# The second transform stage taken four chunks at a time, with its row swaps replaced by other matmuls, and one output tile required between wide groups

## The chip, the cores and the metric

The kernel runs on one core of a Trainium2 chip. The metric is the device time of one execution in microseconds, as a median of several runs. One execution was also recorded by the hardware profiler; its own time stands beside the others in the table below.

## What is computed

Two branches read the same normalized input and are added to it:

```python
xn = _layernorm(x, axis=-1)                      # x: 1 x 2048 x 576
return x + _A_ref(xn, k, v, shift_k, ssm_k, ssm_D) + _B_ref(xn, w1, w2)

# _A_ref: a short causal convolution of k, times v, then a causal convolution
# over all 2048 positions for each of 576 channels, then times xn
kv = k_shift * v
y_f = rfft(pad(kv)) * rfft(pad(ssm_k))
y = irfft(y_f)[:S] + kv * ssm_D
return q * y

# _B_ref
h = jnp.maximum(jnp.einsum("bsd,df->bsf", x, w1), 0)   # 576 -> 4608
return jnp.einsum("bsf,fd->bsd", h, w2)                # 4608 -> 576
```

## The kernel before

**The dense branch is the frame.** It runs in 36 steps called quads (18 blocks of 256 hidden columns, for each of two halves of the tokens). A quad consists of products into two PSUM banks (`psh`, 128 x 512, line 569 for every matmul of this branch) and of eight *units* (`mm2`): twelve matmuls of 288 columns into one of two double banks (`pso`), which VectorE then adds to the accumulator of a token tile (line 749). The values are split into a high and a low part, so each product takes three matmuls of the type fp32r. ScalarE makes the high part of activations (`hh`, line 591) and weights (line 512), VectorE the low part of the activations (`ll`, line 593), GpSimd that of the weights (line 513).

**The convolution branch is a stream beside it.** `conv()` is a generator. After every product and unit, `tick` adds to a clock of the dense branch and, at a rate set by `SHARE` and by the planned costs `W_...` and counts `N_...`, lets the generator run on to its next `yield`. So the place of each convolution step among the dense matmuls is fixed by these numbers when the program is built. A step whose matmuls need four PSUM banks yields "wide" first and then may start only at a tick with `place`, which is one behind a product and not one behind a unit. Two of its banks are `psf` (a pool of two), the other two are lent by `borrowed()`: the double bank of the unit that was closed last (`psg`). VectorE must have added that unit to its accumulator before a matmul may write there.

The long convolution is a transform in two stages of sizes 64 and 32, the product with the transformed filter, and the way back. First the filter (`zk`) and then the input (`zx`) go through the first stage into DRAM; then comes the **second stage**, which the change rewrites; last the output stage reads `zy`.

**The second stage before.** Its data are 36 chunks of 128 rows (2 groups of 32 real and 32 imaginary rows) by 512 columns. It takes them in 18 pairs. The constant `m_sb` is a 64 x 64 matrix, one for the way ahead and one for the way back; `turn` multiplies a pair by it with four matmuls of 64 x 64 x 512, each in its own quarter of TensorE's array. For each pair there are three turns: of the filter (`spectrum`, into `psg`), of the input (into `psf`), and the way back (into `psf`). A product of complex numbers needs each real row beside its imaginary row: ScalarE copies the filter twice (line 1020), four DMAs swap half the rows (line 1025), VectorE multiplies in four operations (line 1047), four DMAs swap half the rows of one product (line 1052), and VectorE joins the two with a sign per row in one operation of 1024 columns (line 1059, `join`). The way back follows one pair later, with two copies by ScalarE (line 1067) and two stores (line 1068). Loads of the next chunks (line 1000) and all the swaps go through the queue of SyncE.

Here a *visit* is a stretch of convolution matmuls (line 762) between dense ones. The first and the second turn of the same pair step stand in one visit, the way back in a visit of its own. All order on TensorE is fixed by `in_turn` and `matmuls`; `here()` places operations of ScalarE and VectorE behind the last ones of the dense branch.

The convolution's matmuls are plain fp32, and each shows in the trace as two MATMUL records.

Of the kernel before, what the change touches and what calls it, by code (L numbers as in the profile page):

```python
# [17 lines left out]
P = 128  # L18
S = 2048
D = 576  # L20
# [28 lines left out]
PAUSE = 16000  # L49
PLAIN = 3  # L50
PAUSES = 7.5
SHARE = 0.935


CW = 512
# [5 lines left out]
W_FB, W_FS, W_FK, W_FX, W_FMK, W_FMX, W_FMB, W_FO = 2.8, 4.1, 2.5, 1.75, 4.0, 3.6, 2.9, 3.9  # L61
CONV_TOTAL = (N_FB * W_FB + N_FS * W_FS + N_FK * W_FK + N_FX * W_FX + N_FM * (W_FMK + W_FMX + W_FMB)
              + N_FO * W_FO)


# [1 line left out]
ROWS = 2 * KS + 8  # L67
REST = ROWS * D
Z, KSO, WT = REST, REST + 4 * CW, REST + 4 * CW + 4 * NH
AREA = WT + 4 * U * P  # L70
# [5 lines left out]
def transform_constants():  # L76
# [16 lines left out]
    back = ahead.T  # L93
    mid = np.tile(np.stack([ahead, back], axis=1), (GR, 1, 1)).astype(np.float32)
    return (fwd.reshape(T, P, U, P), inv.reshape(T, P, U, A1),
            np.ascontiguousarray(mid))

# [2 lines left out]
def h3_ffn_kernel(ctx: ExitStack, tc, x, k, v, shift_k, ssm_k, ssm_D, w1, w2, fwd, inv, mid, out):  # L100
# [39 lines left out]
    def fft_psum():  # L140
        return ps_f.tile([P, 512], F32, tag="f", name="psf")

    slot = {"open": 0, "closed": 0}
# [580 lines left out]
    def mm2(g, b, i):  # L724
# [5 lines left out]
        cols = slice(i * P, (i + 1) * P)  # L730
        ps, slot["closed"] = open_ps.pop((g, t))
        unwritten.discard(slot["closed"])
        for h in range(2):
# [26 lines left out]
    def in_turn(ps, a, m, start, stop):  # L760
        with tc.issue_after(done["pe"].ins):
            done["pe"] = nc.tensor.matmul(ps, a, m, start=start, stop=stop, skip_group_check=True)  # L762

    sides = (slice(0, 64), slice(64, P))

    class Ring:

# [30 lines left out]
    def stages(view, views):  # L798
# [164 lines left out]
        for t in range(T):  # L963
            for n in range(KS + 1):
# [8 lines left out]
                if n == 1 or t == T - 1 and n == KS:  # L973
# [6 lines left out]
                    if n == 1 and 2 <= t + 1 < T:  # L980
# [1 line left out]


        stage["seeded"] = ()
        pairs_n = range(NCH // 2)
        raw = {"k": Ring(*views(0, 2, 2, CW)), "x": Ring(*views(ROWS // 2 * D, 2, 2, CW))}
        m_sb = view(8 * CW, 2, 2 * A2)
        filters = Ring(view(4 * CW, 2, 2, CW), view(ROWS // 2 * D + 4 * CW, 2, 2, CW),
                       view(REST + CW, 2, 2, CW))
        other = view(REST - CW, 2, CW)  # L990
        backs = Ring(*views(REST + 5 * CW, 3, CW))
        nc.gpsimd.dma_start(m_sb, mid)

        def both(z, n):
            return z.rearrange("q t g d -> (q t) (g d)")[
                :, 2 * n * CW:2 * (n + 1) * CW].rearrange("p (k n) -> p k n", k=2)

        def load(z, n, name):
            if n in pairs_n:
                nc.sync.dma_start(raw[name].put(n), both(z, n))  # L1000

        def turn(banks, terms):


            for i, (d, src) in enumerate(terms):
                for k in range(2):
                    for r in range(2):
                        in_turn(banks[k][sides[r ^ k]], m_sb[sides[r], d, :],
                                src[sides[r], k, :], i == 0, i == len(terms) - 1)

        def spectrum(n, banks, copied):

            turn(banks, [(0, raw["k"][n])])
            filt = filters.put(n)

            def leave():
                for c in range(2):
                    for dst, src in copied(filt[:, c]):
                        with here():
                            nc.scalar.activation(dst, src, AF.Copy)  # L1020
                for c in range(2):
                    for r in range(2):
                        a = 64 * r + A2 * c
                        b = 64 * r + A2 * (1 - c)
                        nc.sync.dma_start(filt[b:b + A2, c], filt[a:a + A2, c])
                load(zk, n + 2, "k")

            return leave

        def first_spectrum():  # L1030
            banks = [fft_psum() for _ in range(2)]
            spectrum(0, banks, lambda to: [(to[:, k, :], banks[k]) for k in range(2)])()

        def second_spectrum(n):
            wide = borrowed()
            return spectrum(n, [wide[:, k, :] for k in range(2)], lambda to: [(to, wide)])

        def product_of(n):

            banks = [fft_psum() for _ in range(2)]  # L1040
            turn(banks, [(0, raw["x"][n])])
            filt = filters[n]
            leave = second_spectrum(n + 1) if n + 1 in pairs_n else lambda: None
            for c in (1, 0):
                for k in range(2):
                    with here():
                        nc.vector.tensor_tensor(filt[:, c, k, :], banks[k], filt[:, c, k, :],  # L1047
                                                OP.mult)
                if c:
                    for a in range(0, P, A2):  # L1050
                        b = a ^ A2
                        nc.sync.dma_start(other[b:b + A2], filt[a:a + A2, c])
            leave()
            load(zx, n + 2, "x")

        def join(n):
            filt = filters[n][:, 0]
            with here():
                nc.vector.scalar_tensor_tensor(filt, other, sign, filt, op0=OP.mult, op1=OP.add)

        def way_back(n):
            banks = [fft_psum() for _ in range(2)]
            turn(banks, [(1, filters[n][:, 0])])
            for k in range(2):
                vo = backs.put((n, k))
                with here():
                    nc.scalar.activation(vo, banks[k], AF.Copy)
                nc.sync.dma_start(both(zy, n)[:, k, :], vo)

        for n in range(2):  # L1070
            load(zk, n, "k")
        for n in range(2):
            load(zx, n, "x")
        yield -PAUSE
        first_spectrum()
        yield W_FMK
        for n in range(NCH // 2 + 1):
            if n + 1 in pairs_n:
                yield "wide"
            if n:  # L1080
                join(n - 1)
            if n in pairs_n:
                product_of(n)
            yield W_FMK / 2 + W_FMX
            if n:
                way_back(n - 1)
                yield W_FMK / 2 + W_FMB


        order = [*range(HT, T), *range(HT)]  # L1090
# [78 lines left out]
    def tick(cost, place=True):  # L1169
# [134 lines left out]
```

## Time and profile before

| | |
|---|---|
| median of 3 runs | 1029.08 us (1028.98 to 1030.45) |
| the profiled execution | 1038.15 us, of which 1036.3 us are the span of its instructions |
| mean granted TensorE clock | 0.996 |
| busy: TensorE, VectorE, ScalarE, GpSimd | 1019.9, 702.4, 431.4, 463.6 us |
| second stage: first to last of its matmuls | 672.8 to 920.9 us |
| 690 to 920 us: busy TensorE, VectorE, ScalarE, GpSimd | 228.25, 146.91, 102.18, 83.00 us |
| 690 to 920 us: mean busy share of the DMA engines | 0.81, against 0.56 from 480 to 690 us |
| row swaps by DMA | 144, of 128 KB each |

A row of a timeline gives the start and the length in us, the engine, the line, the operation, its output and input by the program's names, the shape, and how many records were merged; in brackets the idle time before it and what ended that. A row of the groups gives busy time and mean ns of one behind the bar. A row of waits gives the total in us, how often, and the longest. Matmuls overlap, so the distance from one start to the next says what a matmul costs; its length does not.

### The profile page before, as it was taken

Reading aid. Unit: us, or ns where it says so; the run is one execution under the profiler, and the core shown is the slowest. Engines: PE = TensorE matmul, PEld = TensorE weight load, DVE = VectorE, ACT = ScalarE, POOL = GpSimd, SP = SyncE. Lnnn points to the kernel's source line nnn. Section 1 sums busy time; section 2 is a strip of 40 time slices with the busy share of each in tenths; the row PEclk is TensorE's granted clock in tenths of the full one; section 3 lists DMA queues with packets and bytes.
Section 4 is the critical chain, followed back from the end, with each engine's and each line's share of the span. In section 5 each row is a group of like instructions: output and inputs, shape, how many; then the busy total and the mean of one; then the engine's idle time right before and its main releaser. Section 6 shows DMA issues by size and latency. Waiting matters only on the chain.

```text
span 1036.3 us, 17434 instructions
## 1 busy us (share of the span) xinstructions
PE 1019.9 (98%) x6506; PEld 846.6 (82%) x6506; DVE 702.4 (68%) x1075; ACT 431.4 (42%) x770; POOL 463.6 (45%) x502
## 2 busy tenths in 40 slices
PE   8999999999999999989999999999999999999997
PEld 5898999998988888878878888866777777788777
DVE  6787677775565556778787889455666666556764
ACT  7244334443354444434444444544444445332120
POOL 3335444555443555544555455314424245244450
PEclk9999999999999999998999999999999999999999
DMA  7114364479445473379944433677877887757684
GB/s 175 52 49 118 114 162 126 154 216 199 115 127 172 160 245 104 126 216 322 277 139 132 129 103 115 210 221 227 242 212 226 250 256 226 221 177 230 208 259 114
DMA packets 130848, 184.69 MB, mean 178 GB/s; under 512 B 69213, under 2 KB 81631, under 8 KB 129868
## 3 DMA queue, kind: packets, MB, share of 16 engines
q1 hardware_dynamic: 76180, 123.48, 39.9%
q0 software_dynamic: 16048, 52.44, 16.9%
q10 hardware_dynamic: 38536, 7.66, 3.9%
q8 instruction: 51, 0.84, 0.3%
q14 instruction: 33, 0.27, 0.1%
HBM read 119.04 MB, written 45.61 MB: 159 GB/s over the span
## 4 chain that ended last, share of the span: by engine, by line
PE 88%; DMA 4%; DVE 3%; ACT 2%; issue 1%; POOL 1%; ACTq 1%; SPq 0%; DVEq 0%; POOLq 0%
PE pso L569 40%; PE psh L569 34%; PE psf L762 6%; PE psg L762 4%; PE psh_c L569 3%; DMA r<-in_w 2%; DMA zk<-area 1%; DMA acc<-in_x 1%; ACTq L809 0%; DVE area L1047 0%; DVE area L941 0%; DVE area L942 0%; ACT x L291 0%; DMA area<-in_k 0%; DVE sums L525 0%
## 5 line engine op out<-in xcount | busy, mean ns | idle before, releaser
L569 PE MATMUL pso<-w,hh 128*128 128x288 f32 x2304 | 467.9, 296 | 0.0
L569 PEld LDWEIGHTS pso<-w,hh 128*128 128x128 f32 x2304 | 378.1, 188 | 35.9 <-issue 14.8
L569 PE MATMUL pso<-w,ll 128*128 128x288 f32 x1152 | 339.5, 295 | 0.0
L749 DVE TENSOR_TENSOR acc<-pso,acc 128x576 f32<-128x576 f32 x243 | 183.1, 754 | 167.3 <-PE pso L569 166.9
L569 PEld LDWEIGHTS pso<-w,ll 128*128 128x128 f32 x1152 | 216.4, 188 | 0.0
L513 POOL TENSOR_TENSOR wb<-sums,wb 128x512 fp32r<-128x512 f32 x33 | 52.4, 1587 | 251.1 <-ACT wb L512 217.9
L513 POOL TENSOR_TENSOR w<-r,w 128x576 fp32r<-128x576 f32 x72 | 108.2, 1510 | 118.6 <-ACT w L512 118.6
L569 PE MATMUL psh<-xs,wb 128*128 128x512 f32 x396 | 102.7, 394 | 0.0
L569 PE MATMUL psh<-x,wa 128*128 128x512 f32 x396 | 102.5, 394 | 0.1
L569 PE MATMUL psh<-hl,wr 128*128 128x512 f32 x264 | 85.7, 406 | 3.6 <-ACT psh L686 3.1
L569 PEld LDWEIGHTS psh<-x,wa 128*128 128x128 f32 x396 | 72.4, 188 | 15.3 <-ACT psh L648 0.5
L569 PEld LDWEIGHTS psh<-xs,wb 128*128 128x128 f32 x396 | 70.6, 188 | 14.6 <-issue 3.2
L513 POOL TENSOR_TENSOR wa<-r,wa 128x512 fp32r<-128x512 f32 x36 | 56.1, 1558 | 57.2 <-ACT wa L512 57.1
L762 PE MATMUL psf<-area 64*64 64x512 f32 (+10 forms) x664 | 75.2, 489 | 1.6 <-DVE area L1047 1.0
L593 DVE SCALAR_TENSOR_TENSOR ll<-psh,hh 128x512 fp32r<-128x512 f32 x66 | 45.2, 685 | 37.6 <-ACT hh L591 37.2
L686 ACT ACTIVATE psh<-psh 128x512 f32<-128x512 f32 x33 | 19.2, 582 | 116.5 <-DVE u L684 114.6
L569 PEld LDWEIGHTS psh<-hl,wr 128*128 128x128 f32 x264 | 46.3, 189 | 23.0 <-issue 10.5
L591 ACT ACTIVATE hh<-psh 128x512 fp32r<-128x512 f32 x66 | 39.3, 596 | 50.8 <-PE psh L569 50.1
L1020 ACT ACTIVATE area<-psg 128x1024 f32<-128x1024 f32 x34 | 33.0, 1024 | 53.7 <-PE psg L762 53.7
L591 ACT ACTIVATE hh<-p 128x512 fp32r<-128x512 f32 x33 | 20.9, 632 | 81.9 <-PE pso L569 46.9
L569 PE MATMUL psh<-xs,wd 128*128 128x512 f32 x198 | 52.6, 401 | 0.0
L1047 DVE TENSOR_TENSOR area<-psf,area 128x512 f32<-128x512 f32 x72 | 44.7, 682 | 11.6 <-DMA area<-area 8.4
(134 smaller groups left out, 1487.0 us busy)
## 6 DMA issues: line engine op xcount, KB each, us to landing
r<-in_w POOLq DMA_DIRECT2D x70, 288.0 KB, 3.8
area<-area SPq DMA_DIRECT2D x144, 128.0 KB, 4.0
r<-in_w POOLq DMA_DIRECT2D x35, 512.0 KB, 4.8
zk<-area SPq DMA_DIRECT2D x64, 144.0 KB, 2.2
area<-zk SPq DMA_DIRECT2D x18, 512.0 KB, 4.5
area<-zx SPq DMA_DIRECT2D x18, 512.0 KB, 4.1
zy<-area SPq DMA_DIRECT2D x36, 256.0 KB, 4.7
area<-zy SPq DMA_DIRECT2D x32, 288.0 KB, 4.3
```

Source lines behind the costliest of these rows:

```text
L513: nc.gpsimd.tensor_tensor(w[:, 1, :n], src, w[:, 0, :n], OP.subtract)
L569: last = nc.tensor.matmul(ps, a, m, start=start and n == 0, stop=n == len(seq) - 1, skip_group_check=True)
L591: done["act"] = nc.scalar.activation(hh, ps, AF.Relu)
L593: nc.vector.scalar_tensor_tensor(ll, ps, 0.0, hh, op0=OP.max, op1=OP.subtract)
L686: nc.scalar.activation(x, y, AF.Copy, scale=-1.0)
L749: done["acc"] = nc.vector.tensor_tensor(two(acc[t]), ps[:, :, :NH], two(acc[t]), OP.add)
L762: done["pe"] = nc.tensor.matmul(ps, a, m, start=start, stop=stop, skip_group_check=True)
L1020: nc.scalar.activation(dst, src, AF.Copy)
L1047: nc.vector.tensor_tensor(filt[:, c, k, :], banks[k], filt[:, c, k, :], OP.mult)
```

## The change

The second stage takes four chunks at a time, nine times. Real and imaginary rows no longer share a tile: `ahead` makes, for each half of the rows (64 partitions) and each of four chunks, the 32 real results (c = 0) and the 32 imaginary ones (c = 1) with two matmuls of 64 x 32 x 512. The four chunks fill the 128 partitions of a bank, and so the real parts lie in one bank and the imaginary parts in another, for each half. The swaps, the second copy of the filter, `sign` and the DMAs of lines 1025 and 1052 are no longer used. The product is then four multiplications (`times`, for a half) and two additions (`joined`); `way_back` accumulates two matmuls of 32 x 64 x 512 in a bank. The imaginary and real part of the second half of the input are copied to SBUF (`xs`), so that its multiplications read SBUF alone; those of the first half read PSUM. A step of four is spread over eight planned pieces of `W_FM`, and their total, 9 x 8 x 2.625, equals the total before, 18 x (4.0 + 3.6 + 2.9). Loads are twice as large and half as many.

All three kinds of visit (input ahead, filter ahead, way back) now need four banks. `SHARE` goes from 0.935 to 0.942, which moves every step of the stream to slightly later ticks. `tick` lets a wide group start only if a unit has been closed since the last loan.

```diff
-SHARE = 0.935
+SHARE = 0.942
-N_FB, N_FS, N_FK, N_FX, N_FM, N_FO = 23, 14, A2, T * (2 * KS + 1) + 2, NCH // 2, T
+N_FB, N_FS, N_FK, N_FX, N_FM, N_FO = 23, 14, A2, T * (2 * KS + 1) + 2, NCH // 4, T
...
     def borrowed():
+        slot["lent"] = slot["units"]
         return ps_o.tile([P, 2, 512], F32, tag=f"o{slot['closed']}", name="psg")
...
+        def ahead(name):
+            narrow, wide = four_banks()
+            banks = narrow, [wide[:, c, :] for c in range(2)]
+            for c in range(2):
+                for k in range(4):
                     for r in range(2):
+                        in_turn(banks[r][c][quarters[k], :],
+                                m_sb[sides[r], 0, A2 * c:A2 * c + A2],
+                                raw[name][sides[r], k, :], True, True)
+            return narrow, wide
...
+        def times(n, r, x, c):
+            filt = filters[n]
+            to = [spec[:, r, i, :] for i in range(2)] if c == 0 else [filt[:, r, i, :]
+                                                                      for i in range(2)]
+            for i in range(2):
+                with here():
+                    nc.vector.tensor_tensor(to[i], x, filt[:, r, i, :], OP.mult)
+
+        def joined(n, r):
+            filt = filters[n]
+            for i, op in enumerate((OP.subtract, OP.add)):
+                with here():
+                    nc.vector.tensor_tensor(spec[:, r, i, :], spec[:, r, i, :],
+                                            filt[:, r, 1 - i, :], op)
+
+        def way_back(n):
+            narrow, wide = four_banks()
+            banks = [*narrow, wide[:, 0, :], wide[:, 1, :]]
+            for c in range(2):
+                for k in range(4):
                     for r in range(2):
+                        in_turn(banks[k][sides[r], :], m_sb[quarters[k], 1 + c, :],
+                                spec[quarters[k], r, c, :], c == 0, c == 1)
+            leave((back[:, 0:2], back[:, 2:4]), narrow, wide)
...
+        for n in fours:
+            yield "wide"
+            narrow, wide = ahead("x")
             with here():
+                nc.scalar.activation(xs, wide, AF.Copy)
+            load(zx, n + 1, "x")
+            for c in range(2):
+                times(n, 0, narrow[c], c)
+                yield W_FM
+            joined(n, 0)
+            yield W_FM
+            if n + 1 in fours:
                 yield "wide"
+                spectrum(n + 1)
+                yield W_FM
+            for c in range(2):
+                times(n, 1, xs[:, c, :], c)
+                yield W_FM
+            joined(n, 1)
+            yield W_FM * (1 if n + 1 in fours else 2)
+            yield "wide"
+            way_back(n)
+            yield W_FM
...
-        while steps and clock["conv"] >= 0 and (place or not clock["wide"]):
+        while steps and clock["conv"] >= 0 and (
+                not clock["wide"] or place and slot["units"] > slot["lent"]):
```

What this does to TensorE's order is seen in quad 27 of the second stage. These are TensorE's rows before, from a way back (two `psf` banks, four matmuls) to the next input and filter; `psh27_...` are dense products, and the rows of the units `pso26_...` that lie between are marked by dots:

```order
L569 MATMUL psh27_5_7696<-xs1_4842,wc27_7598 128x512 x3
L762 MATMUL psf_7700<-area_1173 64x512 x2
L762 MATMUL psf_7701<-area_1173 64x512 x2
L569 MATMUL psh27_5_7696<-xs1_4842,wc27_7598 128x512 x3
...
L569 MATMUL psh27_5_7696<-hl2_4911,wr27_7532 128x512 x2
L762 MATMUL psf_7751<-area_1173 64x512 x2
L762 MATMUL psf_7752<-area_1173 64x512 x2
L762 MATMUL psg_7757<-area_1173 64x512 x4
L569 MATMUL psh27_5_7696<-xs4_4922,wd27_7529 128x512 x6
```

And TensorE's rows of the changed program in the same quad, from a way back (eight matmuls in two rounds) over one unit to an input ahead, of which the first two rows are shown (lines 571 and 765 are 569 and 762 of before):

```order
L765 MATMUL psf_7584<-area_1173 64x512 x2
L765 MATMUL psf_7585<-area_1173 64x512 x2
L765 MATMUL psg_7583<-area_1173 64x512 x4
L765 MATMUL psf_7584<-area_1173 64x512 x2
L765 MATMUL psf_7585<-area_1173 64x512 x2
L765 MATMUL psg_7583<-area_1173 64x512 x4
L571 MATMUL psh27_1_7536<-hl2_4910,wr27_7500 128x512 x2
L571 MATMUL pso26_10_7563<-w226_7299,hh26_0_0_7281 128x288 x2
...
L571 MATMUL psh27_2_7537<-xs2_4812,wb27_7494 128x512 x6
L765 MATMUL psf_7639<-area_1173 32x512
L765 MATMUL psg_7638<-area_1173 32x512
```

Before, a lent bank (`psg`) was first written in the second turn of a visit, behind the two `psf` banks; in the changed program the second matmul of an input ahead writes it already, and a way back needs it in its first round. In the whole program there were 64 visits, and now there are 55: 27 in place of 36 belong to the second stage.

ScalarE's rows in the changed program behind that way back are these (line 1026 is the copy out of the second stage's banks, 593 makes `hh`, 665 copies a dense bank, 1071 is the copy into `xs`):

```order
L1026 ACTIVATE area_1173<-psf_7584 128x512
L1026 ACTIVATE area_1173<-psf_7585 128x512
L1026 ACTIVATE area_1173<-psg_7583 128x1024
L593 ACTIVATE hh27_0_0_7609<-psh27_1_7536 128x512
...
L1071 ACTIVATE area_1173<-psg_7638 128x1024
```

Before, `hh27_0_0` stood behind two copies of `psf` and two of `psg`, as the following rows of ScalarE before show:

```order
L1067 ACTIVATE area_1173<-psf_7573 128x512
L1067 ACTIVATE area_1173<-psf_7574 128x512
L1020 ACTIVATE area_1173<-psg_7628 128x1024 x2
L591 ACTIVATE hh27_0_0_7651<-psh27_1_7564 128x512
```

VectorE's rows before, at the same place (line 749 adds a unit to its accumulator, 593 makes `ll`):

```order
L1059 SCALAR_TENSOR_TENSOR area_1173<-area_1173,sign_85 128x1024
L1047 TENSOR_TENSOR area_1173<-psf_7622,area_1173 128x512 x2
L1047 TENSOR_TENSOR area_1173<-psf_7623,area_1173 128x512 x2
L749 TENSOR_TENSOR acc10_5124<-pso26_10_7601,acc10_5124 128x576
L593 SCALAR_TENSOR_TENSOR ll27_0_0_7652<-psh27_1_7564,hh27_0_0_7651 128x512
L749 TENSOR_TENSOR acc10_5124<-pso26_11_7655,acc10_5124 128x576
```

And these are VectorE's rows of the changed program there and on to the next way back (line 752 adds a unit to its accumulator, 595 makes `ll`, 1040 is `times`, 1046 `joined`, 693 adds a dense bank):

```order
L595 SCALAR_TENSOR_TENSOR ll27_0_0_7610<-psh27_1_7536,hh27_0_0_7609 128x512
L752 TENSOR_TENSOR acc10_5121<-pso26_10_7563,acc10_5121 128x576
L1040 TENSOR_TENSOR area_1173<-psf_7639,area_1173 128x512 x2
L1040 TENSOR_TENSOR area_1173<-psf_7640,area_1173 128x512 x2
L752 TENSOR_TENSOR acc10_5121<-pso26_11_7613,acc10_5121 128x576
...
L752 TENSOR_TENSOR acc14_5257<-pso26_14_7765,acc14_5257 128x576
L595 SCALAR_TENSOR_TENSOR ll27_0_1_7762<-u2_27_7663,hh27_0_1_7761 128x512
L1046 TENSOR_TENSOR area_1173<-area_1173 128x512 x2
L693 TENSOR_TENSOR p5_27_7711<-psh27_2_7537,p5_27_7711 128x512
L752 TENSOR_TENSOR acc14_5257<-pso26_15_7779,acc14_5257 128x576
```

The accumulation of a unit whose bank is lent next stands here behind `ll`, products and sums of the second stage, in the order of VectorE's queue.

More of the change, by code (lines that the diff above doesn't have):

```diff
@@ L732, in mm2 @@
         unwritten.discard(slot["closed"])
+        slot["units"] += 1
         for h in range(2):
@@ L764, in h3_ffn_kernel @@
     sides = (slice(0, 64), slice(64, P))
+    quarters = [slice(a, a + A2) for a in range(0, P, A2)]
     class Ring:
@@ L984, in stages @@
         stage["seeded"] = ()
[L985 to L991, printed above, removed]
+        fours = range(NCH // 4)
+        raw = {"k": view(0, 4, CW), "x": view(4 * CW, 4, CW)}
@@ L1030, in first_spectrum @@
[L1030 to L1054, printed above, removed]
@@ L1056, in join @@
-        def join(n):
-            filt = filters[n][:, 0]
-            with here():
[L1059 to L1078, printed above, removed]
-                yield "wide"
[L1080 to L1087, printed above, removed]
+            if n in fours:
+                nc.sync.dma_start(raw[name], four(z, n))
@@ new lines, in leave, with spectrum @@
+        def leave(to, narrow, wide):
+            for dst, ps in ((to[1], wide), (to[0][:, 0, :], narrow[0]), (to[0][:, 1, :], narrow[1])):
+                with here():
+                    nc.scalar.activation(dst, ps, AF.Copy)
+        def spectrum(n):
+            filt = filters.put(n)
+            leave([filt[:, r] for r in range(2)], *ahead("k"))
+            load(zk, n + 1, "k")
+        def times(n, r, x, c):
[5 more added lines that the diff above has]
+                    nc.vector.tensor_tensor(to[i], x, filt[:, r, i, :], OP.mult)
```

54 lines of the change are left out of this document (26 added, 28 removed).

## Prediction

> **What bounds the kernel now.** I read the busy times, the chain that ended last, TensorE's timeline in the second stage, and then what the visits there waited for.
>
> ```profile
> span 1036.3 us, 17434 instructions
> PE 1019.9 (98%) x6506; PEld 846.6 (82%) x6506; DVE 702.4 (68%) x1075; ACT 431.4 (42%) x770; POOL 463.6 (45%) x502
> PE 88%; DMA 4%; DVE 3%; ACT 2%; issue 1%; POOL 1%; ACTq 1%; SPq 0%; DVEq 0%; POOLq 0%
> ```
>
> TensorE is the bound from end to end, by its busy time and by the chain. So an edit moves the time by what it adds to or takes from TensorE's own stream: matmuls, the cost of going over to the convolution and back, and waits of a matmul for others. VectorE at 68% has room on average but can be late at a place.
>
> TensorE's timeline in the second stage prices a visit:
>
> ```profile
> 745.70 1.53 PE L569 MATMUL psh<-xs,wb 128*128 128x512 f32 x6
> 747.07 0.42 PE L569 MATMUL pso<-w,hh 128*128 128x288 f32 x2
> ...
> 748.65 0.85 PE L569 MATMUL psh<-xs,wc 128*128 128x512 f32 x3
> 749.44 1.09 PE L762 MATMUL psf<-area 64*64 64x512 f32 x8
> 750.46 0.97 PE L569 MATMUL psh<-xs,wc 128*128 128x512 f32 x3
> 751.26 0.43 PE L569 MATMUL pso<-w,hh 128*128 128x288 f32 x2
> ...
> 754.24 0.62 PE L569 MATMUL psh<-hl,wr 128*128 128x512 f32 x2
> 754.79 1.09 PE L762 MATMUL psf<-area 64*64 64x512 f32 x8
> 755.70 1.04 PE L762 MATMUL psg<-area 64*64 64x512 f32 x8
> 756.67 1.66 PE L569 MATMUL psh<-xs,wd 128*128 128x512 f32 x6
> 758.17 0.43 PE L569 MATMUL pso<-w,hh 128*128 128x288 f32 x2
> ```
>
> Six dense matmuls take 1.37 us from start to start (745.70 to 747.07), a unit 1.58 (747.07 to 748.65). With a visit of one turn between, six take 2.61 (748.65 to 751.26): the visit costs 1.24. Eight dense matmuls with a visit of two turns take 3.93 (754.24 to 758.17); without it they would take 1.83, so it costs 2.10. One more turn thus costs 0.86, and **coming and going 0.38** a visit. A turn streams 512 columns for four matmuls at once, so all four quarters of the array run side by side.
>
> These visits of the second stage cost more than that:
>
> ```profile
> 685.07 1.96 PE L762 MATMUL psf<-area 64*64 64x512 f32 x8
> 686.52 1.36 PE L762 MATMUL psg<-area 64*64 64x512 f32 x8
> 687.81 0.73 PE L569 MATMUL psh<-hl,wr 128*128 128x512 f32 x2
> ...
> 693.96 1.67 PE L762 MATMUL psf<-area 64*64 64x512 f32 x8 [0.85 <-DVE area L1047]
> 695.77 0.74 PE L569 MATMUL psh<-hl,wr 128*128 128x512 f32 x2
> ...
> 705.81 1.09 PE L762 MATMUL psf<-area 64*64 64x512 f32 x8
> ...
> 710.57 0.73 PE L569 MATMUL psh<-hl,wr 128*128 128x512 f32 x2
> ...
> 828.54 2.15 PE L762 MATMUL psf<-area 64*64 64x512 f32 x8
> 830.62 1.66 PE L569 MATMUL psh<-x,wc 128*128 128x512 f32 x6
> ...
> 895.36 1.44 PE L762 MATMUL psf<-area 64*64 64x512 f32 x8
> 896.73 0.97 PE L569 MATMUL psh<-x,wc 128*128 128x512 f32 x3
> ...
> 908.01 2.19 PE L762 MATMUL psf<-area 64*64 64x512 f32 x8
> 910.13 0.96 PE L569 MATMUL psh<-xs,wb 128*128 128x512 f32 x3
> ```
>
> A visit of one turn is left after 1.02 us above, one of two turns after 1.88, one of three after 2.74. Here the differences are 0.86, 1.64 (0.79 and the idle 0.85), 2.02, 1.06, 0.35 and 1.10: **7.0 us of waits in the stage**. Of what they hang on the view of VectorE's waits tells:
>
> ```profile
> DVE area L1047 <- DMA area<-area: 8.4, 4, 3.8
> DVE area L1059 <- DMA area<-area: 1.9, 1, 1.9
> ```
>
> VectorE waited for swaps five times, and with it, one step later, the matmuls that need its results or its banks.
>
> **The change part by part.** *Matmuls.* 54 turns of four become 27 visits of sixteen matmuls. Each quarter of the array is used by two smaller tiles, 64 x 32 or 32 x 64, and eight stand side by side. If they run so, a visit streams 2 x 512 columns: two turns, 1.72 us, and 27 x 2 = 54 turns cost what 54 cost before. No row has such tiles. It cannot cost less, since the columns are the same and the array is full; if only four run at a time, each visit costs 1.72 more, 46 us in all. I take no change, by the nearest row: in 749.44 eight records, with their weight loads, take two passes of 0.43.
>
> [...]
>
> *Visits.* 36 become 27: 9 x 0.38 = **3.4 us less**.
>
> *Swaps.* 144 DMAs go, with the sign and the second copies of the filter. All six waits hang on an order that is gone, so I take out all **7.0** and count below every wait of the new order. If only the first, second and last went, which stand beside VectorE's waits for swaps, it would be 0.86 + 1.64 + 1.10 = 3.6.
>
> *New waits.* A lent bank is free once VectorE has added the unit that filled it. Before, a visit first ran a turn into `psf`, 0.86 us; now it writes the lent bank at once. The prices for VectorE and ScalarE:
>
> ```profile
> L749 DVE TENSOR_TENSOR acc<-pso,acc 128x576 f32<-128x576 f32 x243 | 183.1, 754 | 167.3 <-PE pso L569 166.9
> L1047 DVE TENSOR_TENSOR area<-psf,area 128x512 f32<-128x512 f32 x72 | 44.7, 682 | 11.6 <-DMA area<-area 8.4
> L593 DVE SCALAR_TENSOR_TENSOR ll<-p,hh 128x512 fp32r<-128x512 f32 x33 | 34.3, 1039 | 0.2
> L1059 DVE SCALAR_TENSOR_TENSOR area<-area,sign 128x1024 f32<-128x1024 f32 x18 | 24.0, 1335 | 2.0 <-DMA area<-area 1.9
> 706.93 2.48 DVE L1047 TENSOR_TENSOR area<-psf,area 128x512 f32<-128x512 f32 x4 [0.45 <-PE psf L762]
> 687.92 1.94 ACT L1020 ACTIVATE area<-psg 128x1024 f32<-128x1024 f32 x2 [3.95 <-PE psg L762]
> 696.15 1.08 ACT L1067 ACTIVATE area<-psf 128x512 f32<-128x512 f32 x2
> ```
>
> Three visits of quad 27, by the order of the changed program. (a) Way back to input ahead: TensorE does two matmuls, a unit and six, 0.46 + 1.58 + 1.37 and some 0.2 for coming back, and is there after 3.6. ScalarE copies three banks and makes `hh`, 1.08 + 0.97 + 0.54 = 2.6, VectorE makes `ll` and adds the unit, 0.68 + 0.75: 4.0. Wait 0.4. (b) Input to filter: unit and six, 3.15; VectorE 2.48 + 0.75 = 3.2. Wait 0.1. (c) To the next way back: from the end of unit 14 two matmuls, a unit and six, 3.4; VectorE adds unit 14, makes `ll`, joins twice, adds `p`, adds unit 15: 0.75 + 0.68 + 2 x 0.8 + 0.68 + 0.75 = 4.5. Wait 1.1.
>
> Elsewhere the dense steps between visits stand otherwise. Adding the same rows there, fewer than half of the 27 visits wait, mostly some half a microsecond; I take 0.3 a visit, **8 us**. The price that no row shows is that of an operation of 512 columns that reads SBUF alone, 8 for a four, 72 in all. The rows bound it by 0.68 and 1.04 (both are of 512 columns; the third reads SBUF alone, beside GpSimd's work), and the fourth, 1.34 for 1024 columns out of SBUF, makes 0.67 for half. I take 0.8, near these two. At 0.68 the waits are about 6, at 1.04 about 18; none is the end below.
>
> *Work beside.* VectorE's own sum for a four goes from 2 x (4 x 0.68 + 1.34) = 8.1 to 4 x 0.68 + 8 x 0.8 = 9.1; ScalarE's wide copies go from four to three. Off the bound, both cost only through the waits above.
>
> *Loads.* A load is 1 MB now. The rows nearest are
>
> ```profile
> area<-zx SPq DMA_DIRECT2D x18, 512.0 KB, 4.1
> xs<-ops_s SPq DMA_DIRECT2D x4, 1024.0 KB, 12.8
> ```
>
> It is issued when its buffer's last reader is done and needed a four later, some 248/9 = 27 us; even 12.8 lies under that. Without that cover a visit would wait the whole landing. The first input load has about 20 us behind the last input group of the first stage. Nothing.
>
> *Rate and the rule for wide groups.* They move visits of the other stages by a product or a unit; their number stays 28, and the last one stands behind the same product of the last quad. Nothing, except for one wait:
>
> ```profile
> 463.93 0.63 ACT L512 ACTIVATE wa<-r 128x512 fp32r<-128x512 f32 x1 [5.78 <-DMA r<-in_w]
> 465.64 0.94 PEld L762 LDWEIGHTS psg<-area 64*64 64x64 f32 x16 [3.53 <-ACT acc L742]
> ```
>
> A visit of the first stage waits there for ScalarE, which waits for a weight load. In the changed program it stands two matmuls later in the same quad, so the wait may shrink or stay: up to 4 us less, which I leave to the range.
>
> Sum: -3.4 - 7.0 + 8.0 = **-2.4 us**. On the profiled execution, 1038.15 (span 1036.3 and 1.85 around it), that is 1035.7. It lies 9.07 above the median, which I carry over: 1029.08 - 2.4 = 1026.7.
>
> **The rivals.** (1) *The new waits eat the gain*: 8 to 12 us of them, or the old ones cost less in runs without a profiler. For it: (c) above is long, and the profiled run is slower than the others. Time 1027 to 1031. (2) *VectorE is held up by GpSimd*, slower. The place is `joined` and the second `times`, which read SBUF alone; the price, 1.04 in place of 0.8 each, brings the waits to 18 and the time to 1037. It decides against the change from about 0.95 on, where the waits pass 12.5. Against it: the join of before, SBUF alone too, averaged 1.34 for twice the columns. (3) *Eight tiles do not run side by side*: 46 us more, 1072. (4) *The waits do not come*: the change then gives all its 10.4, 1018.7; the case of the forecast shades into it.
>
> **How the numbers follow.** About 0.2%, or 2.06 us, can be told from no change. Forecast with (4): 0.46, between 1018.5 and 1027; the likeliest time is 1026.7. (1): 0.31. (2): 0.13, from 1031 to 1038. (3): 0.10. So faster 0.46, same 0.31, slower 0.23. The range leaves out (3), the end of (2) and little below: 1018.5 to 1036.
>
> **What would show it.** In the timeline of the changed kernel a visit of 32-column tiles should be left after about 1.9 us; 3.6 would mean rival 3. The waits before visits of the second stage should name VectorE's accumulation (line 752) and add to about 8 us; `joined` and the second `times` should average 0.8. No row of a swap may remain, and the number of convolution visits should be 55. If the stage's visits all cost 2.1 us and the time is still not lower, the loss lies in other stages, and the first place to look at is the wait near 465 us.

## The result and the profile after

The changed kernel takes 1046.91 us in the median (1044.33 to 1050.73), the kernel before 1029.76 in the same set: a ratio of 1.0169 (95% interval 1.0149 to 1.0189). It is **17 us slower**, where 2.4 us less were forecast, and the time lies outside the range.

These lines of the page of the profiled execution after (1044.33 us in all) answer to the first three that the prediction shows.

```profile
span 1042.6 us, 17875 instructions
PE 1021.7 (98%) x6938; PEld 850.5 (82%) x6938; DVE 714.4 (69%) x1094; ACT 422.4 (41%) x757; POOL 463.4 (44%) x502
PE 85%; DVE 8%; DMA 2%; ACT 2%; issue 2%; POOL 1%; ACTq 0%; DVEq 0%; POOLq 0%; SPq 0%
```

Busy times tell little: TensorE is busy for 98% as before. The chain says more: VectorE's share rises from 3% to 8%. But the profile of before was taken in an execution 9 us above its median. A second profile of the same kernel (the run before_again below) fits the median, and is the one to compare with:

```profile
span 1026.7 us, 17434 instructions
...
PE 90%; DVE 3%; issue 2%; ACT 2%; DMA 1%; POOL 1%; ACTq 0%; SPq 0%; POOLq 0%; DVEq 0%
```

Where do the 15.9 us between the spans arise? Both programs run the same 288 dense units in the same order, each with twelve `pso` matmuls. So I count these matmuls in both traces and compare the starts of the same unit, in us:

| unit | before (second profile) | after | later by | what lies ahead of it |
|---|---|---|---|---|
| 96 | 339.67 | 339.64 | 0.0 | start, dense work, most filter groups of the first stage |
| 114 | 401.84 | 408.90 | 7.1 | the last filter groups |
| 192 | 658.89 | 668.16 | 9.3 | the taps and input groups of the first stage |
| 264 | 947.46 | 963.31 | 15.9 | the second stage, which the change rewrites |

More than half is lost before the rewritten stage begins. The largest loss stands in the timeline of the changed kernel around 380 us:

```profile
374.01 0.96 PE L765 MATMUL psf<-area 64*64 64x288 f32 x16
...
375.61 1.16 ACTq L166 DMA_DIRECT2D area<-in_k  x2
375.63 13.17 SPq L891 DMA_DIRECT2D zk<-area  x8
375.75 2.13 POOL L904 DMA_DIRECT2D area<-in_shift_k  x4
376.89 2.20 ACTq L166 DMA_DIRECT2D area<-in_v  x2
379.29 0.96 PE L765 MATMUL psf<-area 64*64 64x288 f32 x16
...
387.55 0.61 DVE L850 COPY area<-psf 128x432 f32<-128x432 f32 x1 [7.09 <-DMA zk<-area]
388.17 0.31 DVE L850 COPY area<-psg 128x144 f32<-128x144 f32 x1
388.53 0.85 PE L571 MATMUL pso<-w,hh 128*128 128x288 f32 x2 [4.87 <-DVE area L850]
```

Read it from the bottom. A dense unit waits 4.87 us for VectorE's copies. The second one (388.17) empties the bank lent to the last filter group (379.29). It stands behind the first one (387.55), which waited 7.09 us for stores of the group before (374.01): both groups use the one buffer `z`. These stores were issued from 375.63, together with the loads of k, v and `shift_k` for the next step of the stage. What it costs beyond the wait is in the table by stretches (busy time per engine, then the granted clock, the busy share of the DMA engines, and GB/s):

```profile
380.00:386.00 6.00, 3.65 (x35) 2.87 (x26) 0.46 (x1) 0.31 (x1) 3.05 (x4) 1.00 1.03 342
386.00:393.00 7.00, 4.47 (x16) 4.18 (x17) 3.25 (x6) 2.89 (x6) 2.77 (x3) 0.51 0.93 302
```

The DMA engines are full (1.03 and 0.93), and TensorE is granted half its clock (0.51) over the end of the wait and on to 393 us. The 4.87 us and half of the 4.5 us from 388.53 on make the 7.1 of the table. In the second profile of before, the last group but one stands at 367.64, ahead of these loads; VectorE waits there for 1.54 us and TensorE not at all:

```profile
362.85 0.96 PE L762 MATMUL psf<-area 64*64 64x288 f32 x16
...
367.64 0.96 PE L762 MATMUL psf<-area 64*64 64x288 f32 x16
369.63 0.61 DVE L846 COPY area<-psf 128x432 f32<-128x432 f32 x1 [1.54 <-DMA zk<-area]
```

The group ahead of it began at 362.85, 4.8 us earlier. In the changed kernel the last two groups are 5.3 us apart. So a short distance between two users of `z` is not enough for the long wait.

In the second stage the visits are cheap, as forecast, but dense matmuls wait. This is the timeline after, at the end of a quad:

```profile
862.27 2.39 DVE L1040 TENSOR_TENSOR area<-area 128x512 f32<-128x512 f32 x2
862.71 1.41 POOL L515 TENSOR_TENSOR wb<-sums,wb 128x512 fp32r<-128x512 f32 x1 [17.85 <-ACT wb L514]
864.08 1.18 POOL L515 TENSOR_TENSOR wd<-r,wd 128x256 fp32r<-128x256 f32 x1
864.59 1.22 DVE L595 SCALAR_TENSOR_TENSOR ll<-p,hh 128x512 fp32r<-128x512 f32 x1
865.22 1.18 POOL L515 TENSOR_TENSOR wr<-r,wr 128x256 fp32r<-128x256 f32 x1
865.73 2.91 DVE L1040 TENSOR_TENSOR area<-area 128x512 f32<-128x512 f32 x2
866.37 1.73 POOL L515 TENSOR_TENSOR wc<-sums,wc 128x512 fp32r<-128x512 f32 x1
868.56 0.68 DVE L595 SCALAR_TENSOR_TENSOR ll<-psh,hh 128x512 fp32r<-128x512 f32 x1
869.33 0.58 ACT L650 ACTIVATE psh<-psh 128x512 f32<-128x512 f32 x1 [4.71 <-DVE ll L595]
869.97 1.43 PE L571 MATMUL psh<-x,wa 128*128 128x512 f32 x4 [2.01 <-ACT psh L650]
```

GpSimd makes four weights in a row, VectorE works out of SBUF alone in the same 6 us, and its operations take 1.2 to 1.5 us each, as a mean of each row, in place of 0.68. The two take turns: VectorE's rows end at 864.66, 865.81 and 868.64, each some 0.55 us after a row of GpSimd. So `ll` (868.56) is late; ScalarE must wait for it before it overwrites the bank, and TensorE waits 2.01 us for ScalarE. The same stall stands near 733 us. A third one, near 936 us, hangs on GpSimd's queue. The chain that ended last (start, length, what) runs there over these pieces:

```profile
929.80 3.99 DMA zy<-area
...
933.81 0.04 POOLq L1110
...
934.91 1.30 POOL wb L515
...
936.88 0.68 POOL wr L515
...
937.61 0.50 PE psh L571
```

Line 1110 loads a matrix of the output stage over a part of the area. It starts when the last store of the second stage (929.80) has landed, and it stands in GpSimd's queue ahead of the weights that TensorE needs.

### The profile page after: what moved, and what is told of

Read it like the earlier page. It is cut to its first block, busy times and chain, and to the rows that moved or that the text cites. A ratio compares the mean times of both kernels' runs of the same rounds, so it can differ in the third digit from the quotient of the medians.

```text
span 1042.6 us, 17875 instructions
## 1 busy us (share of the span) xinstructions
PE 1021.7 (98%) x6938; PEld 850.5 (82%) x6938; DVE 714.4 (69%) x1094; ACT 422.4 (41%) x757; POOL 463.4 (44%) x502
## 4 chain that ended last, share of the span: by engine, by line
PE 85%; DVE 8%; DMA 2%; ACT 2%; issue 2%; POOL 1%; ACTq 0%; DVEq 0%; POOLq 0%; SPq 0%
PE pso L571 39%; PE psh L571 32%; PE psf L765 7%; PE psh_c L571 3%; PE psg L765 3%; DVE area L945 1%; DVE ll L595 1%; PE psw L1214 1%; DMA r<-in_w 1%; DVE acc L752 1%; DMA zk<-area 1%; DVE area L946 1%; DVE area L1040 1%; DVE area L1046 1%; DVE area L950 1%
## 5 line engine op out<-in xcount | busy, mean ns | idle before, releaser
L765 PE MATMUL psf<-area 64*32 64x512 f32 (+10 forms) x800 | 87.7, 506 | 0.2 <-DVE area L1046 0.2
L765 PE MATMUL psg<-area 64*32 64x512 f32 (+12 forms) x792 | 81.7, 501 | 0.2 <-DVE acc L752 0.2
L765 PEld LDWEIGHTS psf<-area 64*64 64x64 f32 (+3 forms) x800 | 27.7, 124 | 37.4 <-issue 30.1
L571 PE MATMUL psh<-x,wc 128*128 128x512 f32 x198 | 51.2, 394 | 0.0
```

The source lines that it names most:

```text
L571: last = nc.tensor.matmul(ps, a, m, start=start and n == 0, stop=n == len(seq) - 1, skip_group_check=True)
```

## The experiments

All times are medians; each set of runs had the kernel before beside it. Expectations stand as they were written before the runs.

**The two kernels again.** No edit.

> The kernel before, unchanged, for a second profile. The first one (1038.15 us) lies 9 us above the median (1029). If its wait near 465 us for a weight load (4.2 us of idle TensorE and 3.4 us by the halved clock behind it) and the one near 525 us (2.7 us) are accidents of that execution, this profile is near 1029 us and has neither of them. If they belong to the kernel, it is near 1038 and has both, and the 9 us come from the profiler.

> The changed kernel, unchanged, for a second profile: 1045 to 1050 us. Theory A (the change's own order causes the stalls): the four stalls of the first profile come back at the same matmuls: near 383 us (5.0 us, clock halved for 6.8 us behind it), 733 (2.2), 868 (2.2, clock halved for 3.4 us) and 935 (2.0, clock halved for 3.4 us). Theory B (accidents of an execution, as perhaps the one near 465 us of before): they stand elsewhere or not at all.

Measured: 1029.73 and 1046.53 us (before in this set: 1029.92). The second profile of before has neither of the two waits near 465 and 525 us; they were accidents of the first. In the second profile of after the stalls stand again at the same matmuls, the first at 8.2 us in place of 4.9, the others within 0.2 us; only the halved clock behind the one near 936 us is missing. The stalls belong to the order of the changed program (theory A), not to one execution.

**The pace alone.** In the changed kernel, and the mirror of it in the kernel before:

```diff
-SHARE = 0.942
+SHARE = 0.935
```

> The changed kernel with the pace of before (SHARE 0.935). Theory A1 (the pace puts the first stage's visits where a buffer waits for its stores, near 383 us): that stall and its halved clock go, 8 us less, about 1038 us; the three stalls of the second stage stay. Theory A2 (VectorE and GpSimd in the second stage cost the time): no change beyond 2 us, about 1046.

> The kernel before with the pace of the changed one (SHARE 0.942). A1: a stall of some 5 us and a halved clock of 6.8 us appear near 383 us, about 1037 us. A2: 1029 us, within 2.

Measured: **1032.43 us** (ratio to before 1.0023, 1.0010 to 1.0035) and **1041.41 us** (1.0104, 1.0086 to 1.0121). The number in one line costs the changed kernel 14 us and the unchanged one 11.5. In the profile of the kernel before at the new pace the stall stands at the same place:

```profile
389.06 0.61 DVE L846 COPY area<-psf 128x432 f32<-128x432 f32 x1 [7.54 <-DMA zk<-area]
389.94 0.85 PE L569 MATMUL pso<-w,hh 128*128 128x288 f32 x2 [8.97 <-DVE area L846]
```

Against 1038 and 1037 in the expectations: the stall is longer than in the first profile, perhaps since the last two groups stand only 2.3 us apart there, and the pace costs in the second stage as well. At the old pace the stall near 936 us is gone too; the two at `psh` L650 stay.

**Which half of the program the pace hurts.** One pace up to the last filter group, the other behind it:

```diff
-SHARE = 0.942
+SHARE, FIRST = 0.942, 0.935
...
-        clock["conv"] += rate * cost
+        clock["conv"] += (rate if "taps" in stage else first_rate) * cost
```

> The changed kernel with the pace of before (0.935) up to the last filter group and 0.942 behind it. Theory F (14 us between 0.935 and 0.942 come for the most part from one place, the last filter groups beside the loads of the tap stage): no stall near 383 us, 1033 to 1037 us. Theory G (the pace costs in the second stage, where it brings VectorE's work against GpSimd's): 1040 us or more.

> The mirror of it: 0.942 up to the last filter group and 0.935 behind it. Theory F: the stall near 383 us and the halved clock behind it are there, 1042 to 1046 us. Theory G: 1033 to 1037 us.

Measured, with the two runs above:

| | 0.935 behind it | 0.942 behind it |
|---|---|---|
| 0.935 up to the last filter group | 1032.43 | 1039.42 |
| 0.942 up to it | 1045.64 | 1046.53 |

The first part alone costs 13.2 us, the second alone 7.0, both 14.1: they don't add, presumably since a delay of the dense matmuls in the first part changes what meets what later. Theory F holds in the first column; pace_early is above its 1033 to 1037, because the places of the second stage count as well (F gave G too little). In pace_late unit 114 starts 7.2 us later than in old_share, and unit 192 12.4 later, so a part of the 13.2 arises behind the filter groups. The wait is 7.14 us:

```profile
389.82 0.85 PE L571 MATMUL pso<-w,hh 128*128 128x288 f32 x2 [7.14 <-DVE area L850]
```

**The loads beside that wait.** At pace 0.942, `shift_k` is loaded from ScalarE's queue, and the first loads are written behind the last filter group:

```diff
-                nc.gpsimd.dma_start(sk[:, -t, :], shift_k[-t:1 - t, :].to_broadcast([P, D]))
+                with here():
+                    nc.scalar.dma_start(sk[:, -t, :], shift_k[-t:1 - t, :].to_broadcast([P, D]))
...
-            if e == A2 - 1:
-                load(0)
...
+        load(0)
         for t in (*range(-1, -KS, -1), 1):
```

> The changed kernel, pace 0.942 kept, with the loads of k, v and shift_k for the tap stage issued from ScalarE behind the copies of the last filter group, instead of beside its visit. Theory C (contention: at this pace the last filter group but one is done while those loads fill the DMA engines, so its stores land late, the one buffer z stays taken, the lent bank of the last group is not copied out and TensorE waits 5 to 8 us, with a halved clock behind it): the stall near 383 us is under 1.5 us, no halved clock behind it, 1033 to 1036 us. Theory S (two visits 5.3 us apart are too close for one buffer, whatever else is loaded): the stall stays at 4 us or more and the time at 1043 to 1047.

Measured: 1042.86 us, and the wait is down to 1.97 us, with 3.4 us of halved clock behind it:

```profile
376.65 1.54 ACTq L166 DMA_DIRECT2D area<-in_k  x1
385.41 0.54 PE L571 MATMUL pso<-w,hh 128*128 128x288 f32 x2 [1.97 <-DVE area L850]
```

Part of the loads still came ahead of the copies of the last group (376.65), so the contention was lessened, not taken away: VectorE's copy still waits 5.40 us for the stores. The wait of TensorE follows the loads, which speaks for C against S, as does the short distance in the kernel before. The time does not bear C out: it is 7 us above the range of C and just below that of S, since unit 114 still starts 4.0 us later than in the second profile of before, and the pace costs behind it too. How much of the last 2 us is the single buffer stays open. A second buffer `z` wasn't tried.

**The rule for wide groups.** Taken out of the changed kernel at pace 0.935, and put alone into the kernel before:

```diff
-                not clock["wide"] or place and slot["units"] > slot["lent"]):
+                not clock["wide"] or place):
```

> The changed kernel at the pace of before (0.935) and without the rule that one unit's matmuls stand between two wide groups. Beside old_share at 1032.4. If the rule only moves a few visits: 1031 to 1034. If it keeps TensorE from waiting for a bank that VectorE still holds (no unit between two lent banks): waits of 1 to 2 us at some visits, 1035 to 1040. If it does harm by pushing visits against GpSimd's work at the end of a quad: 1028 to 1031.

> The kernel before with the rule for wide groups alone. If the rule is harmless where no two lent banks follow one another: 1029 to 1031 us. If it alone moves a filter group beside the loads (as the new pace does): 1040 us.

Measured: **1040.91** and 1029.80 us. On the kernel before, the rule does nothing (ratio 0.9994, 0.9983 to 1.0005). The new stage needs it: without it five times two groups run back to back, and the second waits for ScalarE to copy the banks of the first out, as this row of the waits shows:

```profile
PEld psf L765 <- ACT area L1026: 7.1, 5, 1.6
```

**The joins.** At pace 0.935 the 36 joins are left out; then in other runs they move to GpSimd, all or three of four:

```diff
-                    nc.vector.tensor_tensor(spec[:, r, i, :], spec[:, r, i, :],
+                    nc.gpsimd.tensor_tensor(spec[:, r, i, :], spec[:, r, i, :],
```

> The changed kernel at pace 0.935 without the joins of the products (subtract and add are left out, 36 operations of VectorE). Theory V: both stalls at psh L650 go (4.3 us) and the waits at visits fall by 1 to 3 us: 1025 to 1028 us. Theory B (the stage waits for lent banks and for VectorE's accumulation, the joins fit beside): 1031 to 1033 us.

> The changed kernel at pace 0.935 with the 36 joins on GpSimd in place of VectorE. Theory V1 (leaving the joins out gave 9 us because VectorE was late; a join on another engine gives most of it): the stalls at psh L650 go, 1024 to 1029 us. Theory V2 (GpSimd and VectorE slow each other whenever both work, and GpSimd's joins, about 1.5 us each, delay the weights that it makes or the way back): 1031 to 1042 us.

> The changed kernel at pace 0.935; of the four joins of a four, the two of the first half and one of the second go to GpSimd, one stays on VectorE. Theory V (VectorE's lateness before the head of a quad costs, and all joins on GpSimd lost their gain in the one wait of 3.6 us at 771 us with the halved clock behind it): the stalls at psh L650 fall below 1 us, the one at 771 to 2 us or less, 1025 to 1029 us. Theory B (moving the joins only moves the wait): 1031 to 1035 us.

Measured: without the joins **1023.46 us**, 9.0 below old_share and 0.5% below before (ratio 0.9950, 0.9936 to 0.9964). All on GpSimd: 1032.77 us. Split: 1031.08, level with before (1.0003, 0.9992 to 1.0014). The waits of TensorE for `psh` L650, of the kernel at pace 0.935 and (second row, of its weight loads) without the joins, in us, times, and longest:

```profile
PE psh L571 <- ACT psh L650: 4.0, 2, 2.0
...
PEld psh L571 <- ACT psh L650: 0.6, 2, 0.3
```

So VectorE's joins are what made it late at the head of a quad. As a price of the joins the 9.0 us are an upper bound, since without them the ways back have nothing to wait for either. With the joins on GpSimd the two stalls are gone as well, and up to 757 us that kernel is 3.3 us ahead of old_share (start of unit 216); then one way back waits for a join queued behind a weight, and from shortly before the end of that wait on the clock is halved for 6.8 us:

```profile
769.90 1.85 POOL L515 TENSOR_TENSOR w<-r,w 128x576 fp32r<-128x576 f32 x1
771.71 1.25 POOL L1046 TENSOR_TENSOR area<-area 128x512 f32<-128x512 f32 x1
773.50 1.27 POOL L1046 TENSOR_TENSOR area<-area 128x512 f32<-128x512 f32 x1
774.82 1.12 PE L765 MATMUL psf<-area 32*64 32x512 f32 x3 [3.23 <-POOL area L1046]
```

The split brings the two stalls to 0.9 us each and this one to 0.8, as its theory V said, but gains 1.4 us and not the 3 to 7 of V: its time lies in the range of theory B. Where the rest went was not followed up.

**Products straight from PSUM**, pace 0.935, with the four multiplications of the second half pulled up to the lent bank's visit:

```diff
-            with here():
-                nc.scalar.activation(xs, wide, AF.Copy)
             load(zx, n + 1, "x")
             for c in range(2):
+                times(n, 1, wide[:, c, :], c)
+            yield W_FM
+            for c in range(2):
                 times(n, 0, narrow[c], c)
...
-            for c in range(2):
-                times(n, 1, xs[:, c, :], c)
-                yield W_FM
```

> The changed kernel at pace 0.935 with all eight products of a four taken straight from PSUM (no xs copy by ScalarE); the visits stand where they stood. Theory V (VectorE's operations on SBUF alone take up to twice as long beside GpSimd's, and so the `ll` that ScalarE and TensorE wait for at the head of a quad comes late): 36 stretched candidates less, the two stalls of 2.15 us at psh L650 shrink or go, the waits at visits drop from 6.4 to about 4: 1026 to 1029 us. Theory B (the banks matter more: the lent bank is now held for four products, 2.7 us): 1033 to 1040 us, with waits that name VectorE's products.

Measured: 1042.80 us, 10 above old_share. Theory B, and more than it said: the next unit waits for its bank until VectorE has finished.

```profile
PEld psg L765 <- DVE acc L752: 9.6, 11, 2.7
PE pso L571 <- DVE area L1040: 9.5, 4, 3.0
```

The xs copy, which looks like extra work, is what gives the lent bank back in time.

**A pause of the stream at the end of a quad**, pace 0.935, second stage only:

```diff
+        stage["hold"] = False
...
+        stage["hold"] = stage.get("mid", False)
...
-        while steps and clock["conv"] >= 0 and (
+        while steps and clock["conv"] >= 0 and not stage.get("hold") and (
```

> The changed kernel at pace 0.935; in the second stage the stream stands still from the sixth unit of a quad to the first one of the next, where GpSimd makes four weights in a row, and catches up behind it. Theory V (the joins and products cost because they meet GpSimd's work there): the two stalls at psh L650 (4.3 us) go and hardly an operation of lines 1040 and 1046 takes over 1.0 us: 1026 to 1029 us. Theory B (VectorE's work crowds the visits wherever it stands): the waits at visits grow by as much, 1031 to 1035 us.

Measured: 1034.91 us. The joins now take 689 ns at most and the stalls at `psh` L650 are gone, as V says; but the stream catches up in a bunch, and the way back waits for the joins:

```profile
L1048 DVE TENSOR_TENSOR area<-area x36: 681/684/689, 677.1 to 910.6; 128x512 f32<-128x512 f32 x36
...
PE psf L767 <- DVE area L1048: 5.3, 4, 2.0
```

By its time it is theory B: the lateness moved.

**Two more paces** for the changed kernel, 0.930 and 0.938:

> The changed kernel at a faster pace, 0.930. Theory P (what the pace does is where single visits fall against bursts of loads and against GpSimd's work, so it has no trend): anywhere from 1027 to 1042 us, and a stall over 2 us can be named for what is over 1032. Theory T (a slower stream costs, a faster one gains): below 1031 us.

> The changed kernel at a pace half way, 0.938. Theory T (trend): about 1038 to 1040 us, between 1032.4 at 0.935 and 1046.5 at 0.942. Theory P (places): 1030 to 1034 if the last filter groups still stand ahead of the loads of the next stage, 1042 or more, with the stall near 383 us, if they stand beside them.

Measured: 1034.26 and 1037.03 us. With 1032.43 at 0.935 and 1046.53 at 0.942 there is no straight trend, and none of the four is below before. At 0.938 the wait near 383 us is absent (unit 114 starts 0.8 us ahead of that at 0.935), so the 4.6 us above 0.935 come later, in the profiles in the second stage (unit 192 starts level with that at 0.935, unit 264 5.9 us later): P was right about the place and too low in the time.

## Why the prediction was wrong

**The step that failed first** is "*Rate and the rule for wide groups*": "They move visits of the other stages by a product or a unit; their number stays 28 ... Nothing". For the rule this held (rule_on_before: no change). For the rate it did not: 14.1 us on the changed kernel and 11.5 on the one before. So of the 17 us, some 14 are the pace, and 2.5 are what the rest of the change costs at the old pace. I had counted visits and not looked at what each moved visit waits for. Its buffer, its lent bank and the loads issued beside it stood in the trace of before: VectorE's wait for `zk<-area` there shows how little slack the single buffer had. The only wait that I did follow, near 465 us, was an accident.

**The second** is "*New waits*". Its size was right for what it counted: the 27 visits lose 7.3 us beyond their columns and 0.38 each in the profile after, and 6.5 at the old pace, against 8.0. (The loss is the distance between the dense matmuls around a visit, less their own, the visit's columns at full clock and 0.38.) But I followed VectorE's lateness to the visits alone. The dense matmuls at the head of a quad wait for it too, through `ll` and ScalarE: 2.0 us twice, after as at the old pace, and behind the one near 868 us the granted clock was 0.50 for 3.41 us besides. My price for an operation on SBUF alone was right as a mean, 0.8 against these:

```profile
L1040 DVE TENSOR_TENSOR area<-area 128x512 f32<-128x512 f32 x36 | 29.9, 868 | 0.0
L1046 DVE TENSOR_TENSOR area<-area 128x512 f32<-128x512 f32 x36 | 27.9, 812 | 0.0
...
L1046 DVE TENSOR_TENSOR area<-area x36: 675/684/1780, 690.6 to 920.4; 128x512 f32<-128x512 f32 x36
```

The third row (shortest, median, longest in ns) tells why the mean misleads: most take 684 ns, and a few up to 1780. Of lines 1040 and 1046 together, 14 operations take over 0.9 us in this profile, at the ends of several quads, and each of them overlaps one of GpSimd's weights. Rival 2 named this mechanism, gave it 0.13, and priced it by a mean from which it decides. The timeline at 862 us shows it, with 1.2 to 1.5 us an operation beside GpSimd's weights; the 36 products of line 1040 that read PSUM take 693 ns at most in the same profile. In hold_end, where the joins don't meet that work, the longest of them takes 689 ns.

**"*Work beside*"** set moved work off the bound at nothing but the visits' waits, and the loads of the output stage were not looked at: the one of line 1110 holds up GpSimd's weights (1.8 us, and in the first profile 3.41 us at a granted clock of 0.50). At pace 0.935 it does not.

**What held.** *Matmuls*: eight tiles run side by side. A visit begins at 679.26 and its last pass at 680.58:

```profile
679.26 0.61 PE L765 MATMUL psf<-area 64*32 64x512 f32 x1
...
680.58 0.59 PE L765 MATMUL psf<-area 64*32 64x512 f32 x1
...
681.14 0.53 PE L571 MATMUL pso<-w,hh 128*128 128x288 f32 x2
```

It is left after 1.88 us, the forecast 1.9, so rival 3 is out. *Visits*: 55 in the trace, so 9 fewer, at 0.38 us each by the price of before. *Swaps*: the visits of before lose 6.8 us in the first profile and 5.9 in the second, against 7.0.

Put together at the old pace: -3.4 for the visits, 6.5 - 5.9 for their waits, 4.0 to 4.3 for the dense stalls: +1.2 to +1.5; measured +2.5. Without the joins: the visits' waits fall to 3.2, the dense stalls to nothing, -3.4 + 3.2 - 5.9 = -6.1; measured 1023.46 against 1029.43, also 6.0. That is the case of rival 4, in which the new waits hardly come, though with 6.0 us and not its 10.4; the joins take it. The 2.2 us between units 114 and 192 were not followed up.

## What to carry to other kernels

A number that only shifts when side work is issued is a change to every place it shifts: for each moved step, look up the buffer, the bank and the loads that it will now meet, and run the new pace on the old kernel by itself before crediting or blaming the rest. Follow a busier engine not only to the step that was rewritten but to every operation queued behind it, and price it where it stands, by the stretch and not by its mean. Count the clock with a stall: in the profile after, the wait of 4.87 us came to 7.1 us with the halved clock behind it, and one of 2.01 us was followed by 3.41 us at half clock, which by my estimate (half of 3.41) cost 1.7 us more.

## What the runs showed of the hardware

TensorE's granted clock was 0.50 behind some of its waits and stayed at 1.00 behind others. These are its waits of over 1.4 us between 20 and 1000 us in the first profiles of the two kernels:

| kernel | wait of TensorE, us | ended by | ends at | granted clock of 0.50 |
|---|---|---|---|---|
| after | 4.87 | VectorE, line 850 | 388.53 | 386.06 to 392.89 |
| after | 2.00 | ScalarE, `psh` line 650 | 735.05 | none |
| after | 2.01 | ScalarE, `psh` line 650 | 869.97 | 870.75 to 874.16 |
| after | 1.82 | GpSimd, `wr` line 515 | 937.61 | 939.02 to 942.43 |
| before | 2.86 | ScalarE, `acc` line 742 | 465.64 | 464.87 to 471.70 |
| before | 2.56 | ScalarE, `psh` line 686 | 528.15 | none |

So the length of a wait does not tell: one of 1.82 us was followed by the halved clock, those of 2.00 and 2.56 us were not. The stretches last 3.41 or 6.83 us here. In the profile after they start 484.69 and 68.27 us apart, 142 and 20 times 3.413. With the time cut into steps of that length, counted from 870.75, the surroundings of the two equal stalls differ (the granted clock is the third number from the end):

```profile
867.35:870.75 3.40, 1.39 (x8) 1.04 (x7) 3.40 (x5) 0.58 (x1) 2.51 (x4) 1.00 0.30 90
870.75:874.16 3.41, 3.41 (x28) 1.48 (x34) 1.02 (x2) 0.00 (x0) 0.00 (x0) 0.50 0.29 107
...
730.80:734.22 3.42, 2.25 (x17) 2.01 (x16) 3.42 (x4) 0.00 (x0) 3.42 (x4) 1.00 0.00 0
734.22:737.63 3.41, 2.58 (x30) 1.55 (x38) 1.43 (x3) 0.58 (x1) 0.72 (x2) 1.00 0.59 192
```

The stall that ends at 869.97 lies in one step, with 1.39 us of work of TensorE, and the next step runs at 0.50. The one that ends at 735.05 is split between two, with 2.25 and 2.58 us of work, and the clock stays at 1.00. The other steps ahead of a halved stretch hold 1.01 us of work (382.64 to 386.06) and 1.60 (935.60 to 939.02), and before, counted from 464.87, 1.33 (461.45 to 464.87). But there a step with 1.57 (526.31 to 529.72) was followed by 1.00. So these two profiles show no amount of work that parts the two kinds.
